# A causal seven-tap mix and a routed eight-expert MLP on one core: bands by one DMA, half passes in pairs, w2's low part accumulated, four planes

## The chip, the cores and the metric

The kernel runs on one core of a Trainium2 chip. The metric is the device time of one execution in microseconds. Engines, as the profile names them: PE (TensorE, with PEld for its weight loads), DVE (VectorE), ACT (ScalarE), POOL (GpSimd) and SP (SyncE, which here issues most DMAs).

## The reference

`x` has 8 batches of 3,584 tokens of 192 numbers. Stage one mixes each token with the six before it, with softmaxed weights of its own for each of eight heads (24 columns each). Stage two sends every token with a positive skip score through the expert that its gate logits choose: 192 to 1,024, ReLU, back to 192, scaled by the gate's probability, and adds the result to the token.

```python
w = softmax(weight)                         # 8 heads x 7 taps
out = np.einsum('hk,bskhg->bshg', w, x_unf) # each token and the 6 before it
...
do_compute = x @ w_skip > 0
e_idx = np.argmax(xc @ w_gate, axis=1)
h = np.maximum(xc[mask] @ w1[e], 0.0)
y[mask] = gate_w[mask, None] * (h @ w2[e])
out[do_compute] = xc + y
```

## The kernel before

**Stage one.** A batch lies in SBUF as 30 chunks of 120 tokens with 8 tokens of halo (`xs`, 128 partitions). For each head a band matrix `toep[:, h]` (128 x 120, the seven taps on seven diagonals) is PE's stationary operand, and `conv_head` multiplies it with two halves of 15 chunks (L377) and copies the result from PSUM to `ys` on ACT (L379). Batch 0 is done by `conv_pair` (L390, L394) in the order of the string `START`, as bands and pieces of x come in. The bands are built from seven 0/1 masks `mk` (L168): on DVE with a chain of multiply-adds (L184, L187), on ACT with products (L192) that PE (L203) or POOL (L195 to L198) adds up. 42 small matmuls on ones (L150) run on PE before.

SP's queue is in program order: the taps `wk`, batch 0 of x in five pieces and its last chunk, the router's weights `wrs`, batch 1. The load of batch b + 2 takes the buffer of batch b and follows its convolution.

**Routing.** `router` transposes `ys`, multiplies with skip and gate weights in tiles of 32 columns of the array (L478, L482) and yields logits; `slots` ranks tokens within their expert (L560 to L562 are its matmuls; L561 contracts one row); `invert` turns ranks into lists of token numbers: for eight chunks at a time a one-hot `oa` of the row (L665, one instruction a chunk), `eq`, `ob` (L677), and PE's products (L645). These generators are woven into the convolutions of later batches. The eight experts' weights are loaded by `split_weights` and split into a high and a low f16 part.

**Stage two.** Tokens go through the experts in 61 blocks of 256 (`us` = 2) or 128 (`us` = 1) rows: 8 early blocks (`n < NTAIL`), while the last batch is still routed, then 42 of the experts' lists and 11 that are chosen on the device (weights `wd`). For each block `gather` fetches rows (L832), `prep` scales them and splits them into f16 high and low parts (`yt`: L846 on ACT, two L851 on DVE) and a DMA transpose (L854) lays them out as three planes `m` of 128 contraction rows: high rows 0 to 127; high and low of rows 128 to 191; low rows 0 to 127. `up` is the first product: for each of eight chunks of 128 hidden units five passes, in one PSUM bank for two chunks (`us` = 2) or four; `hh` is the ReLU's f16 value (L880, ACT), `hl` the rest (L882, DVE). `down` is the second: from block `NTAIL` on (`wide`) a pass of 384 columns multiplies `hh` with w2's high and low part side by side (L912) and one of 192 `hl` with the high part (L915); two DVE steps add both halves to the row (L898), which is scattered (L901). Early blocks accumulate three passes of 192 in one place (L927).

```python
seq = ((OW1, 0), (OW1, 2), (OW1 + F, 1), (OW1L, 0), (OW1L + F, 1))
```

Each pair is the place of the weights and the plane; the last pass multiplies w1's low part of 64 rows (laid out twice) with their high and low parts.

The order is the program's: the step `up` of block n + 1 stands before `down` of block n, and the pieces of `prep` for blocks up to three ahead are put between their pieces by `weave`. PSUM's eight banks in this stage: five for `ph`, used in rotation, three for `po`.

Of the kernel before, what the change touches and what calls it, by code (L numbers as in the profile page):

```python
# [17 lines left out]
P = 128  # L18
# [37 lines left out]
XC = ((NG // 2, NG, NG + 7), (NG,))  # L56
START = "57a 01a 57c 01c 57d 01d 23a 23b 46a 46b"
NB1 = 7
EVK = 3
WARM = 42  # L60
# [28 lines left out]
def conv_router_moe(ctx: ExitStack, tc: tile.TileContext, x, weight, w_skip, w_gate, w1, w2, out):  # L89
# [24 lines left out]
    def load_x(b):  # L114
# [9 lines left out]
        cuts = (1, *XC[b], NC - 1) if b < 2 else (1, NC - 1)  # L124
# [10 lines left out]
    wk = const.tile([P, H, KT], F32, name="wk")  # L135
    rt = const.tile([P, R], F32, name="rt")
    toep = const.tile([P, H, R], F32, name="toep")
    scratch = wst.tile([P, 2 * F + NF * D], F32, tag="raw", name="mk")
    mk, *taps = (scratch[:, n * KT * R:(n + 1) * KT * R].rearrange("p (k r) -> p k r", k=KT) for n in range(4))
    wkm = const.tile([P, H], F32, name="wkm")  # L140
# [3 lines left out]
    nc.sync.dma_start(out=wk.rearrange("p h k -> p (h k)"),  # L144
                        in_=bass.AP(weight.tensor, weight.offset, [[0, P], [1, H * KT]]))
# [3 lines left out]
    for _ in range(WARM):  # L149
        nc.tensor.matmul(warm, ones16, ones16, start=True, stop=True)  # L150
    nc.gpsimd.iota(rt, pattern=[[-1, R]], base=-(HALO - KT + 1), channel_multiplier=1,
                   allow_small_or_imprecise_dtypes=True)
    nc.scalar.activation(wkm, ones16[:, 0:H], AF.Exp)
    xs[0] = load_x(0)

# [11 lines left out]
    for k in range(KT):  # L167
        nc.vector.tensor_scalar(out=mk[:, k, :], in0=rt, scalar1=float(k), scalar2=None, op0=ALU.is_equal)  # L168
    nc.vector.tensor_reduce(out=wkm, in_=wk, axis=AX.X, op=ALU.max)
    nc.vector.tensor_tensor(out=wk, in0=wk, in1=wkm.unsqueeze(2).broadcast_to([P, H, KT]), op=ALU.subtract)  # L170
    nc.scalar.activation(wk, wk, AF.Exp)
    nc.vector.tensor_reduce(out=wkm, in_=wk, axis=AX.X, op=ALU.add)
    nc.vector.tensor_scalar(out=wkm, in0=wkm, scalar1=1e-9, scalar2=None, op0=ALU.add)
    nc.vector.reciprocal(out=wkm, in_=wkm)
# [1118 lines left out]
```

## Time and profile before

| | |
|---|---|
| median of 3 runs | 706.81 us (706.45 to 708.69) |
| the profiled execution | 710.46 us, its span 708.7 us |
| PE busy | 661.2 us, 93% |
| DVE busy | 577.3 us, 81% |
| ACT busy | 319.5 us, 45% |
| DMA | 129.43 MB, mean 183 GB/s |

A row of a group of instructions gives line, engine, operation, what it writes and reads, shape and count, then the busy time of the group in us and the mean ns of one, then the idle time before them and what ended it. Matmuls overlap in the pipeline, so the mean of one is longer than the distance between two. Stages are told by stretches of the span, in us from its start.

### The profile page before, as it was taken

The numbers are of one execution on the slowest core, as the hardware profiler recorded it, in microseconds if no ns is written. First come the engines' busy times: TensorE is split into PE (matmuls) and PEld (weight loads), VectorE is DVE, ScalarE is ACT, GpSimd is POOL, SyncE is SP. The second block draws the span as 40 slices with busy tenths as digits, with TensorE's granted clock in tenths as the row PEclk, the third lists the DMA queues.
The fourth block names the chain that finished last, engine by engine and source line by source line (L and its number), as shares of the span: only waits on it lengthen the run. The fifth ranks groups of instructions, "written<-read, shape, count | busy, mean of one in ns | idle before, by whom it ended". The sixth has DMA issues, their size and how long they took to land.

```text
span 708.7 us, 16534 instructions
## 1 busy us (share of the span) xinstructions
PE 661.2 (93%) x5768; PEld 526.2 (74%) x5768; DVE 577.3 (81%) x1856; ACT 319.5 (45%) x654; POOL 303.7 (43%) x430
## 2 busy tenths in 40 slices
PE   5699799997998899999999999999999999999995
PEld 4466466665587888778888888888888888888884
DVE  4508799887899976999988998899899997777763
ACT  3376376684772222354363353443533533343321
POOL 4411110111602345456556555555564655555322
PEclk9899899999999999999999999999999999999998
DMA  7399989984583536356456357257365546999960
GB/s 228 106 312 269 301 261 327 313 255 134 137 268 91 140 83 167 68 167 159 114 165 177 86 168 183 80 163 177 101 178 140 154 103 175 292 267 266 341 175 14
DMA packets 154161, 129.43 MB, mean 183 GB/s; under 512 B 59360, under 2 KB 141026, under 8 KB 154068
## 3 DMA queue, kind: packets, MB, share of 16 engines
q1 hardware_dynamic: 143028, 106.49, 52.2%
q0 software_dynamic: 11040, 21.80, 12.2%
q8 instruction: 47, 0.77, 0.5%
q14 instruction: 46, 0.38, 0.2%
HBM read 69.70 MB, written 48.04 MB: 166 GB/s over the span
## 4 chain that ended last, share of the span: by engine, by line
PE 55%; DVE 1%; issue 0%; DMA 0%; POOL 0%; POOLq 0%
PE ph L877 29%; PE po L912 17%; PE po L915 9%; DVE o L898 0%; DVE wt L331 0%; DMA y<-out_dram,lst 0%; DVE hl L882 0%; DVE yt L851 0%; POOL out_dram L901 0%; POOLq L1220 0%; DVE yam L841 0%; DVE ar L355 0%; DVE yam L350 0%; DVE yam L352 0%; DVE yf L892 0%
## 5 line engine op out<-in xcount | busy, mean ns | idle before, releaser
L877 PE MATMUL ph<-m,wt 128*128 128x256 f16 (+1 forms) x2000 | 221.0, 268 | 5.4 <-DVE hl L882 2.8
L880 ACT ACTIVATE hh<-ph 128x512 f16<-128x512 f32 x230 | 133.1, 592 | 199.9 <-PE ph L877 165.0
L877 PEld LDWEIGHTS <-wt 128*128 128x128 f16 x2000 | 188.5, 98 | 29.8 <-issue 7.7
L882 DVE SCALAR_TENSOR_TENSOR hl<-ph,hh 128x512 f16<-128x512 f32 x230 | 155.9, 686 | 25.5 <-ACT hh L880 21.7
L912 PE MATMUL po<-wt,hh 128*128 128x384 f16 x656 | 167.6, 326 | 1.2 <-DVE o L898 1.2
L915 PE MATMUL po<-wt,hl 128*128 128x192 f16 x656 | 147.5, 246 | 0.0
L912 PEld LDWEIGHTS <-hh 128*128 128x128 f16 x808 | 78.3, 98 | 41.2 <-DVE o L898 1.5
L901 POOL DMA_INDIRECT out_dram<-o,lst x82 | 85.6, 1043 | 52.1 <-DVE o L898 34.0
L832 POOL DMA_INDIRECT y<-out_dram,lst x82 | 89.5, 1091 | 34.2 <-issue 30.6
L846 ACT ACTIVATE yt<-y,ysc 128x192 f16<-128x192 f32 x115 | 46.4, 449 | 90.2 <-issue 33.6
L915 PEld LDWEIGHTS <-hl 128*128 128x128 f16 x808 | 79.0, 98 | 10.2 <-issue 0.2
L377 PE MATMUL pc<-xs,toep 128*120 128x360 f32 x224 | 80.0, 480 | 0.0
L898 DVE SCALAR_TENSOR_TENSOR o<-po,yf,y 128x192 f32<-128x192 f32 x115 | 47.2, 415 | 29.0 <-PE po L912 15.6
L379 ACT COPY ys<-pc 120x720 f32<-120x720 f32 x56 | 42.8, 764 | 44.3 <-PE pc L377 30.1
L851 DVE SCALAR_TENSOR_TENSOR yt<-y,ysc,yt 128x64 f16<-128x64 f32 x230 | 57.9, 312 | 4.2 <-ACT yt L846 2.4
L831 POOL COPY tick<-hh 1x1 f16<-1x1 f16 x104 | 21.2, 203 | 81.6 <-ACT hh L880 74.4
L377 PEld LDWEIGHTS pc<-xs,toep 128*120 128x120 f32 x224 | 37.5, 186 | 14.7 <-issue 1.2
L898 DVE SCALAR_TENSOR_TENSOR o<-po,yf,o 128x192 f32<-128x192 f32 x101 | 42.2, 418 | 3.6
L877 PE MATMUL ph<-m,wd 128*128 128x256 f16 (+1 forms) x440 | 43.4, 258 | 0.0
L331 DVE SCALAR_TENSOR_TENSOR wt<-raw,ar,wt 128x512 f16<-128x512 f32 x56 | 41.6, 744 | 1.9 <-ACT wt L320 1.9
L665 DVE TENSOR_SCALAR oa<-iota_r,rf 120x128 f16<-120x128 f16 x240 | 42.7, 259 | 0.0
L301 DVE TENSOR_REDUCE am<-raw 128x1 f32<-128x512 f32 x56 | 37.8, 676 | 4.5 <-DMA raw<-in_moe_w_dram 4.2
(233 smaller groups left out, 895.7 us busy)
## 6 DMA issues: line engine op xcount, KB each, us to landing
wd<-wscr SPq DMA_DIRECT2D x44, 449.0 KB
xs<-in_x_dram SPq DMA_DIRECT2D x6, 2688.0 KB
out_dram<-ys SPq DMA_DIRECT2D x6, 2436.0 KB
wscr<-wt SPq DMA_DIRECT2D x84, 128.0 KB
raw<-in_moe_w_dram SPq DMA_DIRECT2D x32, 192.0 KB
raw<-in_moe_w_dram SPq DMA_DIRECT2D x8, 512.0 KB
raw<-in_moe_w_dram SPq DMA_DIRECT2D x16, 256.0 KB
wscr<-wt SPq DMA_DIRECT2D x14, 256.0 KB
```

The costliest lines, as they stand in the source:

```text
L377: nc.tensor.matmul(pc[0:R, i, 0:n * G], toep[:, h, :], xs[:, c0 + n * i:c0 + n * i + n, h * G:(h + 1) * G], start=True, stop=True)
L379: nc.scalar.copy(ys[0:R, c0:c1, h * G:(h + 1) * G].rearrange("p (i g) c -> p i g c", i=i1), pc[0:R, 0:i1, 0:n * G].rearrange("p i (g c) -> ...
L832: rows_apart(nc.gpsimd.indirect_dma_start(out=k.y[:, u, :], out_offset=None, in_=out[0:k.rows, :], in_offset=bass.IndirectOffsetOnAxis(ap= ...
L846: nc.scalar.activation(yt[:, u, 0:D], k.y[:, u, :], AF.Copy, scale=sc[:, u:u + 1])
L851: nc.vector.scalar_tensor_tensor(out=yt[:, u, o:o + b_ - a], in0=k.y[:, u, a:b_], scalar=sc[:, u:u + 1], in1=yt[:, u, a:b_], op0=ALU.mult, ...
L877: nc.tensor.matmul(ph[:, f - f0, :], wt[:, o + f * P:o + (f + 1) * P], k.m[:, m, 0:w], start=(n == 0), stop=(n == len(seq) - 1))
L880: nc.scalar.activation(hh, ph, AF.Relu)
L882: nc.vector.scalar_tensor_tensor(out=k.hl[:, f0:f0 + fs, 0:w], in0=ph, scalar=0.0, in1=hh, op0=ALU.max, op1=ALU.subtract)
L898: nc.vector.scalar_tensor_tensor(out=o[:, u, :], in0=part, scalar=f2[:, u:u + 1], in1=base, op0=ALU.mult, op1=ALU.add)
L901: rows_apart(nc.gpsimd.indirect_dma_start(out=out[0:k.rows, :], out_offset=bass.IndirectOffsetOnAxis(ap=k.si[u], axis=0), in_=o[:, u, :], ...
L912: nc.tensor.matmul(po, k.hh[:, f, u * P:(u + 1) * P], w2[:, f], start=(f == 0), stop=(f == NF - 1))
L915: nc.tensor.matmul(po[:, 1], k.hl[:, f, u * P:(u + 1) * P], w2[:, f, 0], start=False, stop=False)
```

## The change

The bands' rows of one partition hold each head's taps in a row of 128 zeros. One DMA reads 120 copies of the 1,024 numbers, each one element further on, into 120 partitions; PE turns them round with a permutation (`turn_bands`), and two copies fill `toep`. The masks, the DVE, ACT and POOL sums and POOL's identity go; the permutation and the identity come from ramps on PE and DVE. Warm-up matmuls are 6 and 66. Batch 0 is loaded in two halves, and the band DMA stands between them in SP's queue. `START` is a plain list of pairs of heads.

```diff
+START = "01a 23a 45a 67a 01b 23b 45b 67b"
+WARM = (6, 66)
...
+            if b == 0 and c0 == 1:
+                bands()
...
+        nc.sync.dma_start(out=scratch[0:R, 0:H * P],
+                          in_=bass.AP(taps_row.tensor, taps_row.offset, [[taps_row.ap[0][0], 1], [1, R], [1, H * P]]))
+
+    def turn_bands():
+        for h0 in (0, 4):
+            pt = ps_tp.tile([P, 4, R], F32, tag="tp", name=f"pt{h0}")
+            for h in range(4):
+                nc.tensor.matmul(pt[:, h, :], shifted[:, h0 + h, :], turned, start=True, stop=True)
+            if h0 == 0:
+                nc.scalar.copy(toep[:, h0:h0 + 4, :], pt)
+            else:
+                nc.vector.tensor_copy(toep[:, h0:h0 + 4, :], pt)
...
-            for c in range(n):
-                nc.vector.tensor_scalar(out=oa[:, c, :], in0=iota_r[0:R], scalar1=rf[:, c0 + c:c0 + c + 1], scalar2=None,
-                                        op0=ALU.is_equal)
+            nc.vector.tensor_tensor(
+                out=oa[:, 0:g], in0=iota_r[0:R].unsqueeze(1).broadcast_to([R, g, P, 2]), op=ALU.is_equal,
+                in1=rf[:, c0:c0 + n].rearrange("p (g v) -> p g v", v=2).unsqueeze(2).broadcast_to([R, g, P, 2]))
```

SP's queue at the start, before (`wk` are the taps, `xs` the batches of x):

```order
L144 DMA wk<-in_weight_dram 128x56
L123 DMA xs_147<-in_x_dram 120x192
L126 DMA xs_147<-in_x_dram 128x6x192
L126 DMA xs_147<-in_x_dram 128x8x192
L126 DMA xs_147<-in_x_dram 128x7x192 x2
L129 DMA xs_147<-in_x_dram 112x192
```

and now (`mk` is the scratch tile that holds the taps' row and the shifted rows):

```order
L144 DMA wk<-in_weight_dram 1x56
L119 DMA xs_121<-in_x_dram 120x192
L122 DMA xs_121<-in_x_dram 128x14x192
L177 DMA mk<-mk 120x1x1024
L122 DMA xs_121<-in_x_dram 128x14x192
L127 DMA xs_121<-in_x_dram 112x192
```

The band DMA, which waits for DVE's taps, stands ahead of the second half of batch 0 and of all that follows.

In `prep` the planes become four: the high part of rows 0 to 63 twice; high 64 to 191; high and low of 0 to 63; low 64 to 191. The weights' two row groups change places accordingly (`split_weights`). In `up`, from block `NTAIL` on, two PSUM banks are opened together, and the fifth pass of a chunk of each, now w1's low part times the high part of 64 rows alone, runs on one half of the array's rows; the low-times-low product of those rows is no longer computed in these blocks. `down` has one form: three passes of 192.

```diff
+        passes = ((OW1, 1), (OW1, 3), (OW1 + F, 2), (OW1L, 1))
...
+        for f0 in range(0, NF, 2 * fs):
+            phs = [opened(f0 + fs * n) for n in range(2)]
+            for i in range(fs):
+                for n in range(2):
+                    r, f = slice(64 * n, 64 * n + 64), f0 + fs * n + i
+                    nc.tensor.matmul(phs[n][:, i, :], wt[r, OW1L + F + f * P:OW1L + F + (f + 1) * P], k.m[r, 0, 0:w],
+                                     start=True, stop=False, tile_position=(64 * n, 0))
+                for n in range(2):
+                    chunk(phs[n][:, i, :], f0 + fs * n + i, passes, True)
+                    if i == fs - 1:
+                        high(phs[n], f0 + fs * n)
+                        yield
+                        low(phs[n], f0 + fs * n)
...
+            nc.scalar.activation(yt[:, u, c:c + D], k.y[:, u, :], AF.Copy, scale=sc[:, u:u + 1])
+            nc.scalar.activation(yt[:, u].rearrange("p (a b) -> p a b", a=2)[:, :, 0:c],
+                                 k.y[:, u, 0:c].unsqueeze(1).broadcast_to([P, 2, c]), AF.Copy, scale=sc[:, u:u + 1])
...
+            nc.vector.scalar_tensor_tensor(out=yt[:, u, c + D + c:], in0=k.y[:, u, :], scalar=sc[:, u:u + 1],
+                                           in1=yt[:, u, c:c + D], op0=ALU.mult, op1=ALU.subtract)
...
-            for part in parts:
-                nc.vector.scalar_tensor_tensor(out=o[:, u, :], in0=part, scalar=f2[:, u:u + 1], in1=base,
-                                               op0=ALU.mult, op1=ALU.add)
-                base = o[:, u, :]
+            nc.vector.scalar_tensor_tensor(out=o[:, u, :], in0=part, scalar=f2[:, u:u + 1], in1=k.y[:, u, :],
+                                           op0=ALU.mult, op1=ALU.add)
```

`chunk` issues the four passes of a chunk on the full array, `high` and `low` are L880 and L882 as functions, `opened` takes the next PSUM bank.

PE in the middle of a block, before: the end of one chunk and the start of the next, all on the full array (`ph` is PSUM, `m` the planes, `wt` the weights):

```order
L877 MATMUL ph_4_6199<-m_5935,wt_4909 128x256
L877 LDWEIGHTS wt_4909
L877 MATMUL ph_4_6199<-m_5935,wt_4909 128x256
L877 LDWEIGHTS wt_4909
L877 MATMUL ph_6_6223<-m_5935,wt_4909 128x256
L877 LDWEIGHTS wt_4909
L877 MATMUL ph_6_6223<-m_5935,wt_4909 128x256
```

and now, where a pair of banks begins (L880 are the two half passes, into the banks `ph_4` and `ph_6`; L856 those on the full array):

```order
L856 MATMUL ph_2_5516<-m_5258,wt_4740 128x256
L880 LDWEIGHTS wt_4740
L880 MATMUL ph_4_5552<-m_5258,wt_4740 128x256
L880 LDWEIGHTS wt_4740
L880 MATMUL ph_6_5553<-m_5258,wt_4740 128x256
L856 LDWEIGHTS wt_4740
L856 MATMUL ph_4_5552<-m_5258,wt_4740 128x256
L856 LDWEIGHTS wt_4740
L856 MATMUL ph_4_5552<-m_5258,wt_4740 128x256
```

Five passes for each chunk become two half passes for two chunks and eight full ones, with a change between halves and the full array before and behind each two.

DVE at the end of a block, before (`o` is the row's sum, `po` PSUM):

```order
L892 SCALAR_TENSOR_TENSOR yf_6099<-yam_5626,wt_4909,lst 128x2
L898 SCALAR_TENSOR_TENSOR o_6098<-po_0_6100,yf_6099,y_2157 128x192
L898 SCALAR_TENSOR_TENSOR o_6098<-po_0_6100,yf_6099,o_6098 128x192
L352 TENSOR_SCALAR sc_6067<-sc_6067 128x2
L898 SCALAR_TENSOR_TENSOR o_6098<-po_1_6124,yf_6099,y_2157 128x192
L898 SCALAR_TENSOR_TENSOR o_6098<-po_1_6124,yf_6099,o_6098 128x192
```

and now:

```order
L863 SCALAR_TENSOR_TENSOR hl_6275<-ph_4_6321,hh_6274 128x512
L863 SCALAR_TENSOR_TENSOR hl_6275<-ph_6_6322,hh_6274 128x512
L895 SCALAR_TENSOR_TENSOR yf_6365<-yam_5832,wt_4740,lst 128x2
L899 SCALAR_TENSOR_TENSOR o_6364<-po_0_6366,yf_6365,y_2000 128x192
L899 SCALAR_TENSOR_TENSOR o_6364<-po_1_6396,yf_6365,y_2000 128x192
```

The second step of each half block is gone.

More of the change, by code (lines that the diff above doesn't have):

```diff
@@ L5 @@
 from concourse import mybir
-from concourse.masks import make_identity
 from concourse._compat import with_exitstack
@@ L132, in conv_router_moe @@
     xs = {}
[L135 to L136 removed]
     toep = const.tile([P, H, R], F32, name="toep")
     scratch = wst.tile([P, 2 * F + NF * D], F32, tag="raw", name="mk")
[L139 to L140 removed]
+    shifted = scratch[0:R, 0:H * P].rearrange("p (h m) -> p h m", h=H)
+    taps_row = scratch[0:1, H * P:H * P + (H + 1) * P]
+    o = (2 * H + 1) * P
+    turned = scratch[0:R, o:o + R]
+    ramp, down_ramp, one_row = (scratch[0:1, o + n * P:o + (n + 1) * P] for n in (1, 2, 3))
+    wk, wkm = const.tile([1, H, KT], F32, name="wk"), const.tile([1, H], F32, name="wkm")
     ident = const.tile([P, P], F32, name="ident")
@@ L148, in conv_router_moe, with warm_up @@
     warm = ps_ms.tile([P, P], F32, tag="ms", name="warm")
[L149 to L153, printed above, removed]
+    def warm_up(n):
+        for _ in range(n):
+            nc.tensor.matmul(warm, ones16, ones16, start=True, stop=True)
+    warm_up(WARM[0])
@@ new lines, in conv_router_moe @@
+    nc.scalar.activation(wkm, ones16[0:1, 0:H], AF.Exp)
+    nc.vector.memset(one_row, 1.0)
+    nc.vector.tensor_tensor_scan(out=ramp, data0=one_row, data1=one_row, initial=0.0, op0=ALU.mult, op1=ALU.add)
+    nc.vector.tensor_scalar(out=down_ramp, in0=ramp, scalar1=-1.0, scalar2=None, op0=ALU.mult)
+    nc.vector.memset(taps_row, 0.0)
+    grid = [ps_tp.tile([P, 4, R], F32, tag="tp", name=f"grid{n}").rearrange("p u r -> p (u r)")[:, 0:P] for n in range(2)]
+    for g, r in zip(grid, (down_ramp, ramp)):
+        nc.tensor.matmul(g, ramp, one_row, start=True, stop=False)
+        nc.tensor.matmul(g, one_row, r, start=False, stop=True)
@@ L212, in conv_router_moe @@
                             fill=0.0, base=0, channel_multiplier=1)
-    iota_r = const.tile([P, P], F16, name="iota_r")
+    iota_r = const.tile([P, P, 2], F16, name="iota_r")
     iota_q = const.tile([P, NE, 2], F16, name="iota_q")
@@ new lines, in opened, with chunk, high @@
+        def opened(f0):
+            return bank(ph_pools).tile([P, 2 * BLK], F32, tag="ph", name=f"ph{k.n}_{f0}").rearrange("p (f w) -> p f w", w=w)
+        def chunk(to, f, seq, begun):
+            for n, (o, m) in enumerate(seq):
+                nc.tensor.matmul(to, wt[:, o + f * P:o + (f + 1) * P], k.m[:, m, 0:w],
+                                 start=(n == 0 and not begun), stop=(n == len(seq) - 1))
+        def high(ph, f0):
+            nc.scalar.activation(k.hh[:, f0:f0 + fs, 0:w], ph, AF.Relu)
@@ new lines, in low @@
+        def low(ph, f0):
+            nc.vector.scalar_tensor_tensor(out=k.hl[:, f0:f0 + fs, 0:w], in0=ph, scalar=0.0,
+                                           in1=k.hh[:, f0:f0 + fs, 0:w], op0=ALU.max, op1=ALU.subtract)
+        if k.n < NTAIL:
+            for f0 in range(0, NF, fs):
+                ph = opened(f0)
+                for f in range(f0, f0 + fs):
+                    chunk(ph[:, f - f0, :], f, passes + ((OW1L + F, 2),), False)
+                high(ph, f0)
+                yield
+                low(ph, f0)
+            return
@@ L930, in down @@
             yield
-        scale()
-        for u in range(k.us):
-            finish_rows(u, po[:, u])
+            if k.n >= NTAIL:
+                if u == 0:
+                    scale()
+                finish_rows(u, po[:, u])
+        if k.n < NTAIL:
+            scale()
+            for u in range(k.us):
+                finish_rows(u, po[:, u])
     blocks = []
```

149 lines of the change are left out of this document (35 added, 114 removed).

## Prediction

> **What bounds the kernel now.** I read the head of the page, then the engines by stage, then the instructions of one block. Columns of a stage row: its length, then PE, weight load, DVE, ACT and POOL busy (with counts), granted clock, DMA share, GB/s.
>
> ```profile
> span 708.7 us, 16534 instructions
> ```
>
> ```profile
> 2.50:12.00 9.50, 3.30 (x31) 3.03 (x29) 2.27 (x13) 0.25 (x1) 2.67 (x12) 1.00 0.97 287
> 12.00:14.50 2.50, 1.78 (x8) 1.81 (x9) 2.46 (x11) 2.32 (x9) 2.10 (x15) 1.00 0.61 114
> 14.50:23.50 9.00, 3.24 (x11) 2.20 (x10) 8.86 (x24) 2.06 (x8) 8.77 (x10) 0.83 1.04 318
> 23.50:36.00 12.50, 12.25 (x42) 7.80 (x41) 3.55 (x19) 5.98 (x8) 3.51 (x12) 0.85 0.01 3
> 36.00:164.00 128.00, 118.14 (x898) 81.26 (x896) 96.92 (x382) 83.38 (x179) 15.28 (x24) 0.97 0.97 295
> 164.00:311.50 147.50, 132.61 (x1343) 109.99 (x1343) 128.31 (x508) 62.32 (x136) 59.31 (x83) 0.99 0.47 130
> 311.50:683.50 372.00, 371.96 (x3233) 305.10 (x3233) 324.05 (x876) 157.75 (x308) 205.68 (x267) 1.00 0.66 176
> ```
>
> Four stages with four limits. To 36 us the kernel loads two batches of x (2.5 to 12 and 14.5 to 23.5) and waits for the bands; from 23.5 to 36 DMA is idle and PE convolves batch 0. From 36 to 164 DMA is full (0.97) and PE nearly so (118 of 128). From 164 to 311.5 PE and DVE share the limit (132.6 and 128.3 of 147.5). From 311.5 on, over half the span, PE never stops: 371.96 of 372. There a PE nanosecond is a nanosecond of the result, and 48 us of DVE slack is worth nothing.
>
> ```profile
> 368.61 4.37 PE ph L877 x40
> ...
> 376.90 4.37 PE ph L877 x40
> ```
>
> ```profile
> L877 PE MATMUL ph<-m,wt 128*128 128x256 f16 x1840 | 211.3, 273 | 5.4 <-DVE hl L882 2.8 <-issue 1.2 <-ACT ys L379 1.1
> ...
> L877 PE MATMUL ph<-m,wd 128*128 128x256 f16 x320 | 36.2, 273 | 0.0
> ...
> L877 PE MATMUL ph<-m,wt 128*128 128x128 f16 x160 | 9.7, 219 | 0.0
> ...
> L877 PE MATMUL ph<-m,wd 128*128 128x128 f16 x120 | 7.2, 219 | 0.0
> ```
>
> The chain of work repeats every 8.29 us: 40 passes of the first product in 4.37, so 0.109 us for each 256 columns (0.427 ns a column), and 3.92 for the second. The groups count the blocks: (1840+320)/40 = 54 of 256 rows and 280/40 = 7 of 128. The eight early blocks hold six and two, so the change's paired form runs in 48 and 5.
>
> **The fifth passes (largest term).** The pair removes one of two passes for every two chunks: four pairs a block, 48x4 = 192 pairs saving at most 0.109, 5x4 = 20 saving 0.055: 22 us, if the two run side by side and nothing else changes. But the array is now split into two halves of 64 rows and put back for each pair. This trace has such splits:
>
> ```profile
> 58.29 0.27 PE L560 MATMUL pr<-oh,ones 120*128 120x240 f16 x1
> 58.49 0.38 PE L561 MATMUL pr<-hist,ones 1*128 1x8 f32 x2
> 58.80 0.31 PE L562 MATMUL pr<-oh,um 120*120 120x240 f16 x1
> ```
>
> ```profile
> 211.70 0.49 PE L877 MATMUL ph<-m,wt 128*128 128x256 f16 x3
> 212.12 0.82 PE L478 MATMUL pl<-ya,wra 128*32 128x240 f32 x13
> ...
> 212.96 0.59 PE L482 MATMUL pl<-yb,wrb 128*32 128x240 f32 x6
> 213.48 0.61 PE L877 MATMUL ph<-m,wt 128*128 128x256 f16 x4
> ```
>
> ```profile
> L482 PE MATMUL pl<-yb,wrb 128*32 128x240 f32 x112 | 9.8, 372 | 0.0
> ```
>
> ```profile
> 34.70 0.47 PE L390 MATMUL pp<-xs,toep 128*120 128x360 f32 x1
> 35.00 1.37 PE L377 MATMUL pc<-xs,toep 128*120 128x360 f32 x4
> ```
>
> Into 32-column tiles: three L877 from 211.70 stream until 212.03 (3x0.109); L478 starts at 212.12, 0.09 later, though passes of one shape follow each other without a gap. Tiles do run at once: the last six L482 take 0.59 where one takes 0.37, so two rounds of three, 0.20 apart, and twice 0.01 between neighbours. (0.20 is the stream of 240 f32 columns: 360 take the 0.30 from 34.70 to 35.00.) Out of it: the last L482 starts at 213.18 (the group's end, 213.55, less 0.37), streams 0.20, and L877 follows at 213.48: again 0.09, and its first pass is 0.01 longer (0.61 for four is 0.28 + 3x0.11). Into rows: L561 contracts one row and runs on a 32-row tile; L560 streams 240 columns in 0.102, ends at 58.39, and L561 starts at 58.49: 0.09 or 0.10. Back out, the second L561 starts 0.13 after the first and L562 0.18 later, for 8 columns: up to 0.15 beyond its own load.
>
> So I price a pair at 0.094 in + 0.01 load + 0.013 between the halves + 0.109 + 0.094 out + 0.01 = **0.33 us against 0.218 for two full passes**, a loss of 0.11; 192 of them 21.5 us. With 128 columns it is 0.28 against 0.11: 20 x 0.17 = 3.3. **Sum +24.8.** Bounds: no gap at all, 0.122 against 0.218, is -19; gaps of 0.15 on the way out add 12, +37. I take 0.09 both ways because both kinds of split show it, the one-row kind included.
>
> The Trainium skill, TensorEngine Tiling (Array Packing), Theoretical Speedup, promises up to 2x where at most 64 rows are contracted; its Key Properties say that changing the tiling mode, not merely the tile, drains the engine. By the first alone this term would be -19, by the second it is a loss; the 0.09 above agrees with the second.
>
> **w2's low part.** One pass of 384 columns and one of 192 become three of 192.
>
> ```profile
> 374.61 0.49 PE L912 MATMUL po<-wt,hh 128*128 128x384 f16 x2
> 374.94 0.33 PE L915 MATMUL po<-wt,hl 128*128 128x192 f16 x2
> 375.10 0.33 PE L912 MATMUL po<-wt,hh 128*128 128x384 f16 x1
> ```
>
> ```profile
> L898 DVE SCALAR_TENSOR_TENSOR o<-po,yf,o 128x192 f32<-128x192 f32 x101 | 42.2, 418 | 3.6
> ```
>
> From the starts, two of 384 columns take 0.33 and two of 192 take 0.16; at 0.427 ns a column and their small fixed part that is 0.163 and 0.082 each, so 0.245 becomes 0.247, 808 times (101 half blocks of eight chunks): **+1.7**. The extra weight load hides, as the two L915 in a row show. The 101 second L898 go: 42 us of DVE in a stage where DVE waits for PE, so nothing, but for the last one, which ends the kernel: **-0.4**.
>
> **Four planes.** One DVE instruction replaces two in each preparation, ACT gets one more, and each transpose moves a third more. PE, busy 371.96 of 372 with blocks prepared three ahead, hides all three; without that cover it would be one ACT step, shorter than the 0.59 quoted next, per 128 rows. Nothing.
>
> **The pairs' PSUM.** Two banks are now opened together and end 0.44 us apart (four passes). Both must be evacuated before the pair after next: one ACT step, then two of DVE's 0.69 in a row, 1.97 us.
>
> ```profile
> L882 DVE SCALAR_TENSOR_TENSOR hl<-ph,hh 128x512 f16<-128x512 f32 x230 | 155.9, 686 | 25.5 <-ACT hh L880 21.7 <-issue 2.7
> ...
> L880 ACT ACTIVATE hh<-ph 128x512 f16<-128x512 f32 x230 | 133.1, 592 | 199.9 <-PE ph L877 165.0 <-issue 24.2 <-remote 7.2
> ```
>
> With my 0.33 the intervening pair of tiles takes 2.4 us: no stall. Without gaps it takes 2.0, and preparation steps queued between the two L882 would stall PE by 0 to 0.2 us a block, 0 to 10 us: that belongs to the rival below.
>
> **Routing.** Eight small comparisons become one.
>
> ```profile
> L665 DVE TENSOR_SCALAR oa<-iota_r,rf 120x128 f16<-120x128 f16 x240 | 42.7, 259 | 0.0
> ...
> L677 DVE TENSOR_TENSOR ob<-eq,val 120x1024 f16<-120x1024 f16 x24 | 16.6, 690 | 0.0
> ...
> L645 PE MATMUL inv<-oa,ob 120*128 120x128 f16 x240 | 20.6, 220 | 7.0 <-DVE ob L677 6.9
> ```
>
> L677 has the new form and size: 24x0.69 + 8x0.56 = 21, so DVE saves 22 us. Half lies in the DMA-bound stage; PE waits for this chain 6.9 us in all. **-4**, between 0 and -9. The moving operand is now read at every second element; L645 already loads its weights so, and 20.6 us is all that could suffer.
>
> **The start.** The bands come by one DMA: 120 rows of 4,096 bytes, 0.49 MB, all read from one SBUF partition, in SP's queue behind the first half of x0 and ahead of its second half and x1.
>
> ```profile
> 10.32 0.23 DVE L169 TENSOR_REDUCE wkm<-wk 128x8 f32<-128x56 f32 x1
> ...
> 11.93 0.22 DVE L175 TENSOR_TENSOR wk<-wk,wkm 128x56 f32<-128x56 f32 x1
> ```
>
> The tap steps took DVE from 10.32 to 12.15 us, 1.83. With wk there by 4 or 5 us (at the latest by 10.3, where DVE used it, which would add 5), the DMA is issued at 6.5 and moves from about 8, when the first half of x0 is in. Behind it the other half needs 4.2 us, the small loads 2.5 (12 to 14.5), x1 9.0, landing 1: batch 1 can start at 24.7 plus the bands' time T. Convolving batch 0 (9.7 us, 32 passes of 0.302) after bands, landing and turning would allow 20 + T, so x1 decides. It now starts at 35.0, so the term is T - 10.3. How long is T? At the full rate, 375 GB/s, 1.3 us. But few partitions are slow to read here: each batch's store ends with the 8-partition piece (174 KB) and a small one.
>
> ```profile
> 141.50:142.50 1.00, 1.00 (x4) 0.39 (x3) 1.00 (x5) 0.43 (x2) 0.00 (x0) 1.00 1.09 375
> 142.50:143.00 0.50, 0.50 (x10) 0.36 (x13) 0.50 (x5) 0.26 (x1) 0.00 (x0) 1.00 0.94 306
> 143.00:144.00 1.00, 1.00 (x24) 0.46 (x14) 1.00 (x7) 0.50 (x1) 0.00 (x0) 1.00 0.50 121
> 144.00:145.00 1.00, 1.00 (x13) 0.87 (x11) 0.36 (x1) 0.82 (x3) 0.00 (x0) 1.00 0.28 60
> 145.00:146.00 1.00, 1.00 (x7) 0.60 (x6) 0.75 (x1) 0.30 (x2) 0.06 (x1) 1.00 0.11 31
> ```
>
> 375 GB/s falls to 121, 60, 31: 212 KB in 3 us, 71 GB/s. At that rate T is 7; if one partition has an eighth of it, 56. The geometric middle is 20; some of the tail is landing, not rate, so I take 15: **+4.7**. In the next stage DMA is the limit, so what is lost or won here stays.
>
> The Trainium skill, SBUF — State Buffer, Door 1, gives 27.2 GB/s for one port of eight partitions; T would be 18 and this term +7.8. The store's tail agrees that few partitions are slow, but no row here shows one alone.
>
> **The sum.** The profiled execution took 710.46 us (span 708.7 and 1.8 around it). 710.46 + 24.8 + 1.7 - 0.4 - 4 + 4.7 = 737.3. That execution is 3.65 above the median of the runs, 706.81: **734**.
>
> **Rivals.**
> - *Bands quick* (T 1 to 7): everything else as above, start -9 to -3: about 722. For it: DMA engines are free, each row is long; against it: the store's tail.
> - *No gap for halves of 64 rows*, the side on which it gets faster: the array need not drain between a full pass and two half passes. Then -19 instead of +24.8, less up to 10 us of PSUM stalls: it decides from 0.055 us a switch downward, since a pair saves 0.11. With quick bands 680, with bands of 15 us 690 to 700. For it: a 64-row split has no row here; against it: the one-row tile shows 0.09 too.
> - *The halves do not overlap at all*: the change doesn't do what it says, 0.11 more a pair, 734 + 21 = 755.
> - *One partition at an eighth of the store's rate*: T = 56, 775.
>
> **Chances.** Slow bands with gaps (734) 0.43; quick bands with gaps (722) 0.23; no gaps, quick bands (680) 0.16; no gaps, slow bands (695) 0.11; no overlap 0.04; T near 56 0.03. The range 686 to 756 holds the first two, the fourth and the fifth, 0.81, with gaps up to 0.15 inside; the likeliest case alone is 724 to 750. A measurement tells 0.3%, 2.1 us, from no change: faster 0.28 (the two cases without gaps, and a little), same 0.04 (between them), slower 0.68.
>
> **What will show it.** Starts of the half passes: 0.09 after the stream before them if I am right, 0 if not; the block's period, 8.29 now, 8.75 forecast, 7.9 without gaps. The band DMA: GB/s near 30 from 8 to 23 us, and the first L377 near 40. If PE waits for DVE or ACT ahead of ph in the long stage, the PSUM step was wrong. A gap-free split would make the whole forecast wrong.

## The result and the profile after

The changed kernel takes **729.22 us** (median of four runs, 728.73 to 729.59), the one before 706.63 beside it (705.53 to 708.69): the ratio is **1.031, 95% interval 1.028 to 1.035**. The forecast was 734, between 686 and 756.

The changed kernel's page begins so:

```profile
span 727.0 us, 17805 instructions
```

By stage (length, then busy PE, weight load, DVE, ACT and POOL with counts, granted clock, DMA share, GB/s):

```profile
9.00:12.00 3.00, 1.14 (x20) 0.96 (x18) 0.00 (x0) 0.00 (x0) 0.20 (x1) 1.00 0.99 49
12.00:17.00 5.00, 0.00 (x0) 0.00 (x0) 0.00 (x0) 0.00 (x0) 4.60 (x23) 0.53 0.87 31
17.00:24.00 7.00, 0.00 (x0) 0.00 (x0) 0.00 (x0) 0.00 (x0) 0.37 (x1) 0.50 0.85 51
26.00:41.00 15.00, 14.71 (x49) 10.11 (x50) 2.75 (x17) 5.87 (x8) 0.69 (x4) 0.77 0.88 257
41.00:170.00 129.00, 119.18 (x883) 81.93 (x882) 83.92 (x260) 82.63 (x175) 16.57 (x26) 0.95 0.95 285
170.00:320.00 150.00, 144.94 (x1518) 121.12 (x1516) 128.15 (x418) 77.69 (x180) 67.32 (x93) 1.00 0.61 154
320.00:702.00 382.00, 382.00 (x3857) 314.02 (x3854) 270.64 (x675) 170.10 (x381) 195.01 (x259) 1.00 0.66 175
```

The DMA engines are busy from 9 to 24 us and move only 31 to 51 GB/s, where x moved at 287 in the first stage of the profile before: the band DMA. PE, DVE and ACT compute nothing from 12 us until it has landed; POOL works for 4.6 us of the stretch from 12 to 17. From 320 us on PE is busy 382.00 of 382, so no wait on PSUM took the place of anything, and DVE fell from 324 of 372 before to 271 of 382 without any use to the end.

PE at the start, from the timeline (start, length, line, count, and in brackets the idle time ahead with what ended it):

```profile
26.29 3.74 PE L184 MATMUL pt<-mk 120*128 120x120 f32 x16 [16.15 <-DMA mk<-mk]
29.82 11.34 PE L382 MATMUL pp<-xs,toep 128*120 128x360 f32 x32
41.00 0.77 PE L372 MATMUL pc<-xs,toep 128*120 128x360 f32 x2
42.29 0.84 PE L372 MATMUL pc<-xs,toep 128*120 128x360 f32 x2 [0.53 <-DMA xs<-in_x_dram]
```

PE waits 16.15 us for the bands, turns them, convolves batch 0 and starts batch 1 (L372) at 41.00, where it was 35.00. Each f32 matmul has two records here. The first half of batch 1's first head runs at once; the second half waits 0.53 us for the second piece of x1 (the load of batch 1).

One block in the chain of work, in the long stage (start, length, what):

```profile
316.64 0.21 PE ph L880 x2
316.86 0.98 PE ph L856 x8
317.84 0.22 PE ph L880 x2
...
320.44 0.98 PE ph L856 x8
321.42 3.96 PE po L912 x48
325.38 0.21 PE ph L880 x2
```

The period is 325.38 - 316.64 = 8.74 us (before 8.29, forecast 8.75). A pair of half passes and its eight full ones take 1.195 us; eight passes at 0.109 are 0.87, so the pair is 0.32 where two full passes took 0.218. The second product is 3.96 where it was 3.92.

The waits of PE in the routing, and the comparison's new form (busy us, mean ns of one):

```profile
PE inv L622 <- DVE ob L653: 2.0, 3, 1.1
```

```profile
L641 DVE TENSOR_TENSOR oa<-iota_r,rf 120x1024 f16<-120x1024 f16 x24 | 16.6, 692 | 0.0
...
L641 DVE TENSOR_TENSOR oa<-iota_r,rf 120x768 f16<-120x768 f16 x8 | 4.4, 547 | 2.3 <-PE inv L622 2.3
```

42.7 us of DVE became 21.0, as forecast, and PE's waits for `ob` 6.9 became 2.0.

Since both programs run the same blocks in the same order, the start of each product can be held against its counterpart. The distance between the two profiles grows and shrinks so (us, after less before):

| place, time before | distance | what lies between |
|---|---|---|
| batch 1 starts, 35.00 | +6.0 | start |
| last convolution, 193.7 | +5.8 | DMA-bound stage |
| first block, 195.6 | +5.2 | |
| ninth block, 275.5, the first with half passes | -1.6 | routing, early blocks: -6.8 |
| second product of the last two blocks, 695.9 | +19.7 | half passes, second product: +21.2 |
| end of the span, 708.7 | +18.3 | last step and what follows it |

The profiled execution of before was 710.46 us, 3.8 above the median beside which the new one stands, and that of the changed kernel 0.5 below its own: 18.3 + 3.8 + 0.5 is the 22.6 between the medians. By its period and the half passes of the 128-row blocks the part from the ninth block on should be 24.8 (48 x 0.45 + 5 x 0.65); the profile of before lost some 3 us of its own there, between 280 and 320 us, where its PE waits for DVE, `issue` and a plane's DMA come to 3.0.

### The profile page after: what moved, and what is told of

It reads as the page before. It is cut to its first block, busy times and chain, and to the rows that moved or that the text cites. A ratio compares the mean times of both kernels' runs of the same rounds, so it can differ in the third digit from the quotient of the medians.

```text
span 727.0 us, 17805 instructions
## 1 busy us (share of the span) xinstructions
PE 687.5 (95%) x6608; PEld 551.2 (76%) x6608; DVE 496.3 (68%) x1397; ACT 342.0 (47%) x755; POOL 292.0 (40%) x418
## 4 chain that ended last, share of the span: by engine, by line
PE 64%; DVE 0%; ACT 0%; POOL 0%; POOLq 0%; issue 0%
PE po L912 29%; PE ph L856 28%; PE ph L880 6%; DVE o L899 0%; POOL out_dram L901 0%; DVE hl L863 0%; POOLq L1210 0%; ACT hh L860 0%; ACT yt L823 0%; PE pt L674 0%; ACT yt L824 0%; DVE yam L817 0%; DVE ysc L350 0%; ACT rt L670 0%; DVE yam L345 0%
## 5 line engine op out<-in xcount | busy, mean ns | idle before, releaser
L860 ACT ACTIVATE hh<-ph 128x512 f16<-128x512 f32 x230 | 125.6, 587 | 236.6 <-PE ph L856 235.5
L856 PE MATMUL ph<-m,wt 128*128 128x256 f16 (+1 forms) x1664 | 207.0, 269 | 0.8 <-ACT ys L374 0.5
L912 PE MATMUL po<-wt,hh 128*128 128x192 f16 x1536 | 194.3, 246 | 0.0
L912 PE MATMUL po<-wt,hl 128*128 128x192 f16 x768 | 188.9, 246 | 0.0
L856 PEld LDWEIGHTS <-wt 128*128 128x128 f16 x1664 | 143.1, 98 | 35.1 <-issue 2.1
L912 PEld LDWEIGHTS <-hh 128*128 128x128 f16 x1840 | 166.4, 98 | 1.1
L912 PEld LDWEIGHTS <-hl 128*128 128x128 f16 x920 | 90.0, 98 | 0.0
L372 PE MATMUL pc<-xs,toep 128*120 128x360 f32 x224 | 80.7, 483 | 0.5 <-DMA xs<-in_x_dram 0.5
L374 ACT COPY ys<-pc 120x720 f32<-120x720 f32 x56 | 42.7, 762 | 44.8 <-PE pc L372 30.9
L829 DVE SCALAR_TENSOR_TENSOR yt<-y,ysc,yt 128x192 f16<-128x192 f32 x115 | 46.0, 414 | 8.6 <-ACT yt L823 8.4
L372 PEld LDWEIGHTS pc<-xs,toep 128*120 128x120 f32 x224 | 37.7, 188 | 15.9 <-issue 2.0
L880 PE MATMUL ph<-m,wt 64*128 64x256 f16 (+1 forms) x336 | 47.1, 277 | 0.0
L824 ACT ACTIVATE yt<-y,ysc 128x128 f16<-128x128 f32 x115 | 44.4, 386 | 0.0
L856 PE MATMUL ph<-m,wd 128*128 128x256 f16 (+1 forms) x352 | 41.0, 259 | 0.0
```

The lines of the kernel that those rows point to most:

```text
L372: nc.tensor.matmul(pc[0:R, i, 0:n * G], toep[:, h, :], xs[:, c0 + n * i:c0 + n * i + n, h * G:(h + 1) * G], start=True, stop=True)
L824: nc.scalar.activation(yt[:, u].rearrange("p (a b) -> p a b", a=2)[:, :, 0:c], k.y[:, u, 0:c].unsqueeze(1).broadcast_to([P, 2, c]), AF.Cop ...
L829: nc.vector.scalar_tensor_tensor(out=yt[:, u, c + D + c:], in0=k.y[:, u, :], scalar=sc[:, u:u + 1], in1=yt[:, u, c:c + D], op0=ALU.mult, o ...
L856: nc.tensor.matmul(to, wt[:, o + f * P:o + (f + 1) * P], k.m[:, m, 0:w], start=(n == 0 and not begun), stop=(n == len(seq) - 1))
L860: nc.scalar.activation(k.hh[:, f0:f0 + fs, 0:w], ph, AF.Relu)
L880: nc.tensor.matmul(phs[n][:, i, :], wt[r, OW1L + F + f * P:OW1L + F + (f + 1) * P], k.m[r, 0, 0:w], start=True, stop=False, tile_position= ...
```

## The experiments

All programs but the last are the changed kernel with one edit, or full_fifth with one edit. They ran on three occasions after that of the result, on three chips; the kernel before had 708.6, 712.8 and 711.7 us beside them, so ratios to it are compared, and profiles of one occasion where there are such.

### full_fifth, pairs_full: is it the split of the array, or the two banks?

In full_fifth the condition that picks the early form is true for every block:

```diff
-        if k.n < NTAIL:
+        if True:
             for f0 in range(0, NF, fs):
```

> The fifth passes run on the full array in every block, one bank at a time, as in the eight early blocks; all else is the changed kernel. In its profile a pair of half passes costs 0.3225 us (period 1.195 less eight full passes of 0.109) where two full ones take 0.218, with 256 columns, and 0.27 against 0.11 with 128. Theory A (the array's change between halves and full costs the time): 192 x 0.1045 + 20 x 0.158 = 23.2 us less, 729.2 - 23.2 = 706, block period 8.74 - 4 x 0.1045 = 8.32. Theory B (the time is not in the pairs but in the preparation, the start and the second product): 725 to 729.

In pairs_full the two banks stay together and only the half passes become full ones:

```diff
-                    nc.tensor.matmul(phs[n][:, i, :], wt[r, OW1L + F + f * P:...], k.m[r, 0, 0:w],
-                                     start=True, stop=False, tile_position=(64 * n, 0))
+                    nc.tensor.matmul(phs[n][:, i, :], wt[:, OW1L + F + f * P:...], k.m[:, 2, 0:w],
+                                     start=True, stop=False)
```

> Two banks are opened together and evacuated as in the changed kernel, but each of the two half passes is a pass of 128 rows on the full array. Theory A (only the split of the array costs): 706, the same as with the fifth pass in each bank by itself, within 1 us. Theory C (opening two banks together delays PSUM's evacuation and PE waits for it): 715 to 729, with PE waiting for ACT or DVE ahead of ph.

Measured: 704.0 us, ratio 0.995 (0.992 to 0.997), and 705.8, ratio 0.996 (0.993 to 0.999). The chain of full_fifth, then of pairs_full:

```profile
402.63 4.37 PE ph L856 x40
407.00 3.96 PE po L899 x48
410.96 1.09 PE ph L856 x10
```

```profile
407.44 0.22 PE ph L880 x2
407.66 0.87 PE ph L856 x8
408.54 0.22 PE ph L880 x2
```

Full_fifth's period is 8.33. In pairs_full the two passes at L880 take the same 0.22 us as the two halves did, but they do the work of two full passes, and the eight behind them take 0.87 in place of 0.98: the 0.1 us a pair lies in the changes of the array's shape alone, and opening two banks costs nothing that shows. The changed kernel's 729.2, measured on the occasion of the result, lies 25.2 us above full_fifth and 23.4 above pairs_full; theory A said 23.2. By the profiles the half passes are worth 22.6 to 22.8: from the ninth block to the end the changed kernel takes 453.1 us and both others 430.3 to 430.5. The rest of the 25.2 is not theirs: at the first block, up to which the programs are the same, the changed kernel's profile is already 2.9 us behind that of full_fifth and 1.0 ahead of that of pairs_full.

### unpaired, two_groups: more changes, and fewer

In unpaired each half pass goes directly ahead of its own chunk's four full passes:

```diff
-                for n in range(2):
                     chunk(phs[n][:, i, :], f0 + fs * n + i, passes, True)
```

> Each half pass stands alone ahead of the four full passes of its chunk, so that nothing runs beside it and the array is split twice as often. Theory A with overlap (the two halves of a pair do run at once): a lone half costs 0.096 + 0.109 + 0.103 + 0.011 = 0.319, two 0.638 against 0.3225 for a pair; 192 x 0.316 + 20 x 0.26 = 66 us more, about 795, block period 10.0. Theory E (the halves of a pair do not overlap, so that only the splits are added): 192 x 0.21 + 20 x 0.21 = 45 more, 774.

Measured: 795.0 us (one run), as theory A with overlap said (theory E: 774). Its chain:

```profile
404.25 0.21 PE ph L880
404.46 0.54 PE ph L856 x4
405.00 0.21 PE ph L880
405.21 0.54 PE ph L856 x4
```

One half pass alone takes the 0.21 us that two take in the changed kernel. So the halves of a pair do run at once, and what they cost is the change in and out.

In two_groups blocks of 256 rows open four banks, put four half passes next to each other, and then run the full passes of four chunks:

```diff
+        if k.us == 2:
+            phs = [opened(f0) for f0 in range(0, NF, fs)]
+            for i in range(fs):
+                for n in range(4):
+                    half(phs[n][:, i, :], n % 2, fs * n + i)
+                for n in range(4):
+                    chunk(phs[n][:, i, :], fs * n + i, passes, True)
+                    if i == fs - 1:
+                        high(phs[n], fs * n)
+                        low(phs[n], fs * n)
+                    if n % 2:
+                        yield
+            return
```

> In blocks of 256 rows four banks are opened and two pairs of half passes stand next to each other, so that a block has two splits of the array in place of four; blocks of 128 rows are left as they are. Theory A: two pairs together take 0.096 + 2 x 0.109 + 0.103 + 0.011 = 0.43 us where two single ones took 0.645; 48 blocks x 2 x 0.215 = 20.6 us less, 708.6, block period 8.31. Theory D (a pass of 64 rows is itself slow, whatever stands beside it): no change, 729. Theory C (banks opened together stall PE): a part is given back, 712 to 720, with PE waiting ahead of ph.

Measured: 742.4 us, ratio 1.049 (1.042 to 1.056): slower than all three theories. The timeline of PE in an undisturbed block, the largest of PE's waits (in total, times, longest), and three stretches of a disturbed one:

```profile
383.95 0.39 PE L877 MATMUL ph<-m,wt 64*128 64x256 f16 x4
384.28 1.92 PE L856 MATMUL ph<-m,wt 128*128 128x256 f16 x16
386.13 0.39 PE L877 MATMUL ph<-m,wt 64*128 64x256 f16 x4
386.46 1.92 PE L856 MATMUL ph<-m,wt 128*128 128x256 f16 x16
```

```profile
PE ph L877 <- DVE hl L863: 20.5, 20, 2.3
```

```profile
371.00:374.30 3.30, 0.81 (x7) 0.20 (x4) 3.27 (x8) 0.76 (x2) 2.52 (x4) 1.00 0.37 110
374.30:378.00 3.70, 3.70 (x21) 2.20 (x20) 1.80 (x6) 1.38 (x4) 2.35 (x3) 0.57 0.55 133
378.00:382.00 4.00, 4.00 (x44) 3.70 (x43) 2.52 (x6) 2.06 (x4) 1.32 (x2) 0.97 0.08 22
```

The undisturbed block takes 392.27 - 383.95 = 8.32 us (the next begins at 392.27), where A said 8.31: half the changes, half their price. But in some blocks PE stands ahead of the next four banks until those of the block before are emptied. All four end close together, and where an expert's weights are split at the same time ACT comes to them late: ahead of the block shown it had been idle for 3.96 us behind a preparation step that waited for DVE's `ysc`. A halt of 2.3 us costs more than itself: the granted clock is 0.57 in the 3.7 us behind it, and this block takes 12.79 us, 4.5 longer. A and C are both right, and C is the larger: two pairs side by side halve the price of the changes, and with five banks for `ph` the stalls cost more than that. Other numbers of banks were not tried.

### old_oa, wide_w2, old_start: the other parts undone

old_oa has the eight comparisons back (`oa` and `iota_r` as before). wide_w2 has the second product of before from the ninth block on, with two steps at L898. old_start has masks, sums, `START` and the five pieces of batch 0 as before. Their diffs are those parts of the change with the signs exchanged.

> The changed kernel with one comparison a chunk again (eight instructions and 22 us of DVE more). Between 195 and 315 us the changed kernel gained 7.4 us on the one before, in spite of 0.45 a block lost to the half passes from 280 on. Theory J (the single comparison brought it): 733 to 738, and PE waits for ob some 5 us more. Theory K (the steps saved in preparation and at the end of a block brought it): 729 to 730.

> The changed kernel with the second product of before from the ninth block on: one pass of 384 columns and one of 192, and two DVE steps for each half block. The changed kernel's 48 passes take 3.96 us a block where the 32 of before took 3.92. Theory L (PE's own time decides, DVE's 42 us are hidden): 50 x 0.04 = 2 us less, less 0.4 for the last step: 727 to 728. Theory K (DVE's steps were on the path between 280 and 320 us): 730 to 733.

> The changed kernel with the start of before: masks, sums on DVE, ACT and POOL, batch 0 in five pieces, the old order of pairs. Everything else stays. Theory I (what the start loses is carried to the end): batch 1 starts at 35.0 in place of 41.0, 6 us less, 723. Theory H (the DMA-bound stage or the routing behind it swallows the start): 728 to 729.

Measured, in ratios to before: old_oa 1.046 (1.042 to 1.050; 745.7 us), wide_w2 1.031 (1.026 to 1.035; 733.5), old_start 1.025 (1.020 to 1.029; 730.3). The changed kernel itself had 1.031 beside other runs and, on a third occasion, 1.040 (below), so the three are best compared with each other. Two stages of old_oa, and then of wide_w2, which has the new comparison:

```profile
41.00:170.00 129.00, 118.28 (x888) 81.22 (x889) 96.82 (x380) 82.70 (x175) 15.19 (x24) 0.97 0.96 291
170.00:320.00 150.00, 133.71 (x1345) 108.64 (x1343) 123.29 (x474) 66.73 (x158) 58.26 (x81) 0.97 0.51 131
```

```profile
41.00:170.00 129.00, 119.21 (x892) 82.39 (x892) 86.48 (x264) 82.72 (x178) 15.40 (x24) 0.96 0.97 289
170.00:320.00 150.00, 139.79 (x1402) 111.81 (x1401) 124.79 (x410) 73.80 (x173) 63.12 (x88) 1.00 0.53 145
```

Up to the ninth block these two programs differ in the comparison alone (with the layout of `oa` and the place where its generator is interrupted). The ninth block starts 10.2 us later in old_oa (3.9 at the first block, 6.2 more up to the ninth): theory J, and more than it said. In the second stage both keep DVE equally busy, but without the eight comparisons that time is spent on work that PE waits for, and PE does 6 us more in the same stretch.

Of the 10.2 us only the 6.2 are clear of chance; the medians, 12.3 us apart with some 2 of it from the second product, leave room for part of the rest. Five profiles of the result's and the first occasion (after, full_fifth, pairs_full, two_groups, unpaired) are of programs that are the same up to the ninth block; their first blocks start between 197.9 and 201.9 us, but from the first block to the ninth all take 73.0 to 73.1. The seven profiles of the later two occasions with the new comparison, whatever their start, take 76.0 to 77.7, old_oa 82.4, and the kernel before 79.9. DVE's time for the comparison in that stretch, before and after (length, DVE busy, clock, DMA share, GB/s):

```profile
195.60:275.50 79.90, 12.96 (x74) 1.00 0.51 147
```

```profile
200.80:273.90 73.10, 6.01 (x10) 1.00 0.62 166
```

DVE has 6.95 us less to do there and the stretch is 6.8 us shorter, although PE's waits for `ob` in it fell by 1.3 us alone (1.9 to 0.6). Ahead of the first block the comparison takes 14.8 us less (29.73 to 14.97), and the distance between before and after shrinks by 0.8.

Of wide_w2 the end can't be read to 2 us, since the changed kernel did not run beside it; in the long stage its distance to the changed kernel shrinks by 0.04 us a block, as theory L said. Whether DVE's second steps cost something between 280 and 320 us (theory K) stays open.

The first convolutions of batch 1 in old_start, and in wide_w2, which has the new start:

```profile
35.17 1.37 PE L377 MATMUL pc<-xs,toep 128*120 128x360 f32 x4
```

```profile
40.06 0.77 PE L372 MATMUL pc<-xs,toep 128*120 128x360 f32 x2
43.27 0.84 PE L372 MATMUL pc<-xs,toep 128*120 128x360 f32 x2 [2.44 <-DMA xs<-in_x_dram]
```

4.9 us apart there, 4.5 at the first block, and still 4.5 at 297 us: what the start loses is kept (theory I). Behind that the two differ in the second product too.

### four_rows, three_queues: why is the band DMA slow?

In the changed kernel's packet records most of the 120 rows of 4,096 bytes take 2.2 to 2.3 us each, up to 15 of them at a time, and all together, 0.49 MB, move from 7.47 to 25.74 us: 27 GB/s. four_rows (full_fifth with this edit) puts the taps' row in all partitions and reads it from four:

```diff
-        nc.sync.dma_start(out=scratch[0:R, 0:H * P], in_=bass.AP(taps_row.tensor, ...))
+        for j in range(4):
+            row = scratch[32 * j:32 * j + 1, H * P + 30 * j:]
+            nc.sync.dma_start(out=scratch[30 * j:30 * j + 30, 0:H * P],
+                              in_=bass.AP(row.tensor, row.offset, [[row.ap[0][0], 1], [1, 30], [1, H * P]]))
```

> Fifth passes on the full array as in full_fifth (704.0), and the taps' row stands in all partitions, so that four band DMAs of 30 rows each read it from partitions 0, 32, 64 and 96. Theory F (reading one partition is what limits the band DMA): its 17 us become 4 to 6, batch 1 starts about 12 us earlier, first convolution of batch 1 at 27 to 29 in place of 39.6, and the whole is at 692. Theory G (rows of 4,096 bytes from SBUF to SBUF are slow wherever they come from, 1.95 us a packet): no change, 704. Theory H (the bands come sooner, but the stage behind, full with DMA, takes it back): 698 to 704 with the first convolution of batch 1 near 28.

Measured: 718.0 us, ratio 1.008 (1.006 to 1.010). PE's timeline:

```profile
23.95 3.74 PE L186 MATMUL pt<-mk 120*128 120x120 f32 x16 [14.21 <-DMA mk<-mk]
```

The bands land 2.3 us earlier, far from theory F's 12, and the whole was slower than full_fifth had been on another occasion. But the packet records showed both kinds: 37 of the 120 rows at 2.2 to 2.4 us, and 11, of the same size, at 0.159 us, which is 26 GB/s for one row alone. In the changed kernel no row is faster than 0.73. G can't give the quick ones. F can, if four DMAs of one queue are worked off one behind the other, so that most engines still read the same partition and one that is ahead reads the next alone; the records do not name a row's partition, so this is inferred. three_queues lets SP, ACT and POOL issue one of 40 rows each:

```diff
+        for j, q in enumerate((nc.sync, nc.scalar, nc.gpsimd)):
+            row = scratch[32 * j:32 * j + 1, H * P + 40 * j:]
+            q.dma_start(out=scratch[40 * j:40 * j + 40, 0:H * P],
+                        in_=bass.AP(row.tensor, row.offset, [[row.ap[0][0], 1], [1, 40], [1, H * P]]))
```

> full_fifth with the band DMA in three, of 40 rows each, read from partitions 0, 32 and 64 and issued by SP, ACT and POOL at once, so that three partitions are read at the same time; in four_rows four DMAs stood in one queue and most packets still took 2.3 us, while some took 0.16. Theory F (16 engines share what one partition gives, 28 GB/s, and a single engine alone is as fast): the 17 us become about 6, bands land near 14 in place of 26, batch 1 starts at 30 to 33 in place of 39.6 to 41, and the whole is 6 to 9 us below full_fifth on the same chip. Theory G (a row of 4,096 bytes that starts off the 64-byte grid is slow from any partition): packets stay at 2 us and the whole within 1 us of full_fifth. Theory H (the DMA-bound stage takes it back): batch 1 starts near 32, the end is 0 to 3 us earlier.

> The same program as full_fifth, beside the changed kernel and two others on one chip, since four_rows, which differs from it at the start alone, came out 1.3% above it on another chip, with 6 us in which PE waits for its own instructions that full_fifth did not show. Theory M (it was the chip): wherever it runs, 0.966 of the changed kernel on the same chip (704.0 of 729.2). Theory N (the later order of DMAs, moved by the start, costs it): 0.995 of the kernel before, as on the first chip, also if before is at 712 there.

> The changed kernel itself, so that the undone parts can be held against it on one chip. Theory M: its ratio to before is 1.031 on a chip where before takes 706 to 709, and 1.031 to 1.037 on one where it takes 712.

Measured on one occasion: three_queues 715.5 us, ratio 1.005 (1.002 to 1.008); full_fifth_2 720.4, 1.011 (1.008 to 1.015); the changed kernel 739.1, 1.040 (1.036 to 1.044). PE in three_queues, and in full_fifth_2:

```profile
22.26 3.74 PE L186 MATMUL pt<-mk 120*128 120x120 f32 x16 [11.73 <-DMA mk<-mk]
...
35.99 0.77 PE L374 MATMUL pc<-xs,toep 128*120 128x360 f32 x2
38.90 0.84 PE L374 MATMUL pc<-xs,toep 128*120 128x360 f32 x2 [2.14 <-DMA xs<-in_x_dram]
```

```profile
26.27 3.74 PE L184 MATMUL pt<-mk 120*128 120x120 f32 x16 [16.50 <-DMA mk<-mk]
...
40.60 0.77 PE L372 MATMUL pc<-xs,toep 128*120 128x360 f32 x2
```

All 120 packets together keep 16 engines busy for 6.3 us in place of 14.6, as F says. The landing gains only 4.0 us, since SP's third of the rows waits in its queue behind x0 and is read last (packets from 11.2 to 21.8 us), and batch 1's first head then waits 2.14 us for x1. At the end 2.9 us are left in the profiles and 4.9 in the medians. F holds for the engine time; the order of SP's queue now bounds the start. G on the 64-byte grid fails too: of 120 rows that start 4 bytes apart at most 8 begin on that grid, and 23 took 0.16 to 0.2 us. Two things stay open: three_queues changed the queues and the partitions together, and no run reads one partition from three queues; nor does a run tell one partition from a group of its neighbours.

The same program took 704.0 us on the first occasion and 720.4 on the third, the changed kernel 729.2 and 739.1, before 708.6 and 711.7: theory M holds in so far as the place where it runs matters, but its constant ratio of 0.966 does not (0.975 on the third occasion). What differs is this, in PE's waits of full_fifth_2 (in total, times, longest), with the granted clock at 0.50 from 264.2 to 267.5 us behind the longest of the second row:

```profile
PE po L899 <- issue: 6.8, 13, 1.2
...
PE ph L856 <- DVE hl L863: 2.3, 2, 2.0
```

On the first occasion full_fifth had no `issue` wait there and 0.3 us of the other. "issue" is time in which the trace shows nothing that PE waits for. Behind the other row stands ACT: its L860 in that block starts 4.0 us after the block's first pass, in full_fifth 1.3. That wait goes with the occasion and not with the program: seven of the eight profiles of the later two occasions have one of 2.0 us, the changed kernel's own second profile among them, while its first profile has 0.3. What causes it stays open.

### best

The single comparison, four planes and full fifth passes, with the start of before, and the second product of before from the fifteenth block to the last but one:

```diff
+        if NTAIL + 6 <= k.n < NBLK - 1:
+            w2 = wt[:, OW2:OW2 + 2 * NF * D].rearrange("p (l f d) -> p f l d", l=2, f=NF)
```

> What has paid so far, put together: the single comparison in the routing, four planes, fifth passes on the full array, the start of before, and second products with w2's parts side by side from the fifteenth block to the last but one (two DVE steps are then hidden; before it and in the last one pass of 192 at a time). Theory A with I and L: full_fifth less 5 to 6 us for the start and 1.7 for the second product, 697 where full_fifth takes 704, 0.985 of before. Theory H (the start is swallowed behind): 702.

Measured: 706.6 us, ratio **0.992 (0.990 to 0.995)**, on the same occasion as full_fifth_2's 720.4: faster than both kernels there, and 13.8 below full_fifth_2 where 7 were expected. best ran on this occasion alone. Of PE's waits for `issue` the largest row is now at `ph`:

```profile
PE ph L879 <- issue: 2.5, 5, 1.2
```

The two profiles are 11.8 us apart. By their block starts 3.9 of it come from the start, 2.3 from 200 to 330 us and 5.6 behind. 40 blocks x 0.04 explain 1.6 of the 5.6; most of the rest goes with PE's `issue` waits at `po`, which behind 330 us are 3.7 us in full_fifth_2 and 0.5 in best. The second product of 128 rows in passes of 192 columns has 24 passes and 24 weight loads in 1.98 us, the one of before 16 and 16 in 1.96; that PE's instructions then arrive too late is argued, not shown.

## Why the prediction was right, and where it was not

- **Fifth passes, +24.8: right, in mechanism and size.** The change takes 0.096 us in and 0.103 out by the starts of the passes (0.094 was taken for both), the halves start 0.003 us apart (not 0.013), and a pair costs 0.3225 (0.33). That is 192 x 0.1045 + 20 x 0.158 = 23.2. In the profiles of the first two occasions the part from the ninth block on is 22.6 to 22.8 us shorter without it; in medians the difference was 25.2 across these occasions and 18.7 on the third, where full_fifth_2 lost more to `issue` waits than the changed kernel. The forecast had no row for a split into 64 rows, and the one-row tile's 0.09 stood in for it well. The Trainium skill's rule in TensorEngine Tiling (Array Packing), Key Properties, that a change of the tiling mode drains the engine, agrees with these starts.
- **The rival without gaps** is refuted by the same starts, **the rival without overlap** by unpaired: a lone half takes as long as two.
- **Pairs' PSUM, 0 with gaps: right.** PE is busy 382.00 of 382. two_groups shows what happens where four banks end together: the stall that was priced at 0 to 0.2 us a block reaches 2.3 us, and its block is 4.5 longer.
- **w2's low part, +1.7: right in PE's time** (3.96 for 3.92 in a block, 2.0 over all). The step "the extra weight load hides" is not wrong, but on the third occasion, with PE's `issue` waits, passes of 192 seem to have cost up to three times that.
- **Four planes, 0:** nothing in any run speaks against it; it wasn't tried by itself.
- **Routing, -4 (0 to -9): the mechanism right, the size too small.** The forecast started from PE's direct waits for `ob`, 6.9 us. From the first block to the ninth the profiles gained 6.8 us, and old_oa lost 6.2 against wide_w2 there (10.2 with what lies ahead, which is not clear of chance). In a stage where DVE is busy 128 of 147 us its time came back in full, 6.8 for 6.95, and not only at the one wait that names it; that it came back through the early blocks' preparation and the PSUM steps, which stand in the same queue, is argued. In the DMA-bound stage 14.8 us of DVE brought 0.8. This term is the largest error, some 2 to 3 us, and up to 6 if all of the 10.2 counts; 6.8 lies in its range.
- **Start, +4.7: right to 1.3 us, in part by luck.** T was to be 15: the DMA was issued at 5.83, moved from 7.5 and landed near 26, some 18 us. With that the forecast's own sum gives 43.0 for batch 1 and +8.0. Two things stand against each other. From the landing at 25.7 to the second piece of x1 at 42.3 are 16.6 us, where the forecast had 16.7, so the chain by way of x1 was right; but the first half of batch 1's first head needs only the first piece, and starts as soon as batch 0's convolutions end, at 41.0. Those were to allow 20 + T = 38: with PE idle from 10 to 26 us its clock was 0.50 until after 32, so that turning the bands took 3.5 us and the convolutions 11.2 and not 9.7. In the eight other profiles with this start (all but old_start, best and the two with a split band DMA) the convolutions end between 39.6 and 40.6, and PE then waits 0.8 to 2.6 us for x1, until 41.6 to 43.3: there x1 does decide. That the loss stays was right (+6.0 at 35 us, +5.8 at 194, +5.2 at the first block). The Trainium skill's figure in SBUF — State Buffer, Door 1, 27.2 GB/s for one port of eight partitions, would have given T = 18 (an estimate from that page); the 27 GB/s of the band DMA agree with it.
- **The sum.** Against its own execution 26.8 us more were forecast and 18.3 came: 1.3 more from the start, 0.8 less in the stage behind it, 2.8 less from the routing, 1.7 less from the passes, 0.9 less behind the last block, and 3.6 less through waits between 280 and 320 us that the earlier execution had. The waits are about as large as the 3.65 us that were taken off for the median; that they are what set that execution above its median is not shown. The errors of the terms have both signs, so that 734 lies closer to 729.2 than the routing term alone would.

## What to carry to other kernels

A split of the array into row tiles is a change of shape that PE pays for twice, 0.2 us in all; it pays where what runs between two changes saves more than that, so gather small passes before splitting, and count the PSUM banks which that keeps open. A DMA that reads one partition moved 27 GB/s here with up to 15 rows under way at a time, and what stood behind it in the queue waited too. Where an engine was busy for most of a stage, its saved time counted there in full, even if few waits named it (6.8 us for 6.95); where DMA was the limit, it counted for next to nothing (0.8 for 14.8).

## What the runs showed of the hardware

- DMA engines that read one SBUF partition together, with up to 15 rows under way at a time, moved 27 GB/s (0.49 MB in 18.3 us; most rows of 4,096 bytes took 2.2 to 2.3 us each). The quickest rows of four_rows and three_queues took 0.159 us, 26 GB/s, whatever the 4-byte shift of their start; that no other engine read their partition just then is inferred.
- Half passes on rows 0 to 63 and 64 to 127 start 3 ns apart, and two pairs next to each other need no new change (four halves from 383.95, full passes at 384.28).
- PE's granted clock was 0.50 from 13 to 32 us, with PE idle from 10 to 26; 0.57 for 3.7 us behind a halt of 2.3 us at 372 (two_groups); and 0.50 from 264.2 to 267.5 behind a wait of 2.0 us (full_fifth_2). These waits cost more than their length.
- One program differed by 16 us (704.0 and 720.4) between two occasions on two chips, while the kernel before differed by 3: a ratio from one occasion is good for that occasion.
